# A cached attention block with a dense branch, one core: the first unit of work moves into the loop, and the query weights are loaded at other places

## The chip, the cores and the metric

The kernel runs on one core of one Trainium2 chip. The metric is device time in microseconds (us), the median of several executions. Each run is also profiled once; the profiled execution has its own time, and a span from its first to its last instruction. A core has a matrix engine (PE, with its weight loads as PEld), a vector engine (DVE), an activation engine (ACT), a general engine (POOL) and a queue engine (SP) that issues transfers. Sixteen DMA engines carry out the transfers.

## The reference

Shapes: 8 sequences of one token each, width 512, 32 query heads and 8 key/value heads of 128, 8192 cached positions, hidden width 1792, all in float32.

```python
xn = layernorm(x)                                   # no weights
q  = (xn @ wq) in 32 heads of 128
k, v = each of the 8 cached heads, repeated for 4 query heads
scores = einsum("bhqd,bhkd->bhqk", q, k) * 128 ** -0.5
o  = einsum("bhqk,bhkd->bhqd", softmax(scores), v)  # 8 x 4096
h  = xn @ w1 + b1
act = h * tanh(softplus(h))                         # Mish
out = x + o @ wo + act @ w2
```

The caches are 268 MB each; with `wq`, `wo`, `w1` and `w2` the core has to read about 561 MB.

## The kernel before

**Units.** A unit is one sequence `b` and one pair `m` of key/value heads. There are 32, with `m` outside and `b` inside: unit number `u = 8*m + b`. Each has 8 MiB of keys and 8 MiB of values, loaded by one transfer each, 64 KiB to each of 128 partitions. In the program the work of a unit is:

- `scores`: 32 matmuls of the unit's keys with `wk` (queries spread over the partitions by `key_weights`), in two halves. Between the halves SP is given the load of the next unit's keys.
- `softmax` (DVE, ACT and one small PE matmul), then `values`: 32 matmuls on the values of the unit *before*, with its probabilities `pt8`; then SP is given the load of this unit's values.
- `key_weights` for the next unit, `turn` (PE and DVE bring the probabilities into the layout of `pt8`), and `merge` (the output of the unit before is put into `oT`).

**Places.** All of it goes through one tile, `kv`, of 2.5 rows of 64 KiB a partition. Values have row 0 (`V_AT`); keys of even units have row 1 (`K_AT[0]`), keys of odd units the stretch from 1.5 to 2.5 (`K_AT[1]`), so the two key places share half a row. A key load can start when the scores have read that shared half, which is why the halves are in another order in odd and even units. A value load can start when `values` is through with row 0. All these transfers are issued by SP, in order, and each waits for its place.

**Query weights.** `wq` comes in four pieces of 2 MiB, one for each `m`, into the tile `ws`. `project` makes the queries of 8 units from it (PE, ACT, DVE), `spread` lays them out (DVE, PE, ACT). Both run in odd units, for the next `m`: `project` in units 5, 13 and 21, `spread` in units 7, 15 and 23. The loads of the pieces (`load_q`) are issued by SP behind the value loads of units 4, 12 and 20.

**Order.** The schedule is written out by hand: instructions stand on each engine's queue in the order of the code. A prelude normalises `x`, projects the first queries, and works unit 0 in straight code, with its keys in the values' place (row 0) and `w1` in row 1; `up`, the first product of the dense branch, stands in it too. Then a loop of 16 passes follows. Pass `t` works the odd unit `2t+1` (`unit(t, 0, more)`) and the even unit `2t+2` (`unit(t, 1, more)`); in the last pass `last()` takes the place of the even unit. Parts that belong to some passes only stand under `tc.If`, which is a test and a jump on every engine. `mish`, the activation, runs in pass 0 with `ws` as scratch.

Of the kernel before, what the change touches and what calls it, by code (L numbers as in the profile page):

```python
# [8 lines left out]
F32 = mybir.dt.float32  # L9
# [4 lines left out]
P = 128  # L14
# [41 lines left out]

V_AT = 0
K_AT = (ROW, ROW + ROW // 2)
W1_AT = ROW
W2_AT = 2 * ROW  # L60
PLACES = 2 * ROW + ROW // 2

# [4 lines left out]

LOOPS = UNITS // 2  # L70
FAR = 3.0e38


# [3 lines left out]
def kernel(  # L77
# [72 lines left out]
    for lo in range(0, FG, FG // 2):  # L150
        hi = lo + FG // 2
        nc.scalar.dma_start(b1_sb[:, lo:hi], b1.rearrange("(g f) -> g f", g=G)[:, lo:hi])
    nc.sync.dma_start(kv[:, V_AT : V_AT + ROW], kT[:NB].rearrange("j p f -> (j p f)").rearrange("(p f) -> p f", p=P))
    w1_t = kv[:, W1_AT : W1_AT + 7168].rearrange("p (i f) -> p i f", i=W1R)


# [153 lines left out]
            nc.scalar.copy(qr[:, at].rearrange("p i c -> p (i c)"), X[:, half])  # L310

    wk = const.tile([P, DI, 2, NH * G, REP], F32, name="wk")
    lsel = const.tile([P, 2, H2], F32, name="lsel")
    qT = const.tile([P, H2 * B], F32, name="qT")

# [11 lines left out]
            )  # L327


    def scores(j, k, first, part):  # L330

        w = wk
        lo = 0 if first else DI // 2
        kk = k.rearrange("p (i c f) -> p i c f", i=DI, c=HALF)
        for n in range(DI // 2):
            i = lo + n
            for c in range(HALF):
                nc.tensor.matmul(  # L338
                    S[64 * c : 64 * (c + 1), :],
                    w[:, i].rearrange("p d k h -> p (d k h)"),  # L340
                    kk[:, i, c, :],
                    start=(part == 0 and n == 0),
                    stop=(part == 1 and n == DI // 2 - 1),
                )

    E, RT = {}, {}

    def softmax(j):
        nm = work.tile([P, 1], F32, name="nm")
# [11 lines left out]
    def turn(j):  # L361
        e = E.pop(j)
        for g in range(4):
            nc.tensor.matmul(X[:, g], perm[:, g], e, start=True, stop=True)  # L364
        if j % 2 == 1:

            n = 2 * H2
            nc.tensor.matmul(  # L368
                M[:, 136 : 136 + n], ones, lsel.rearrange("p u h -> p (u h)"), start=True, stop=True
            )  # L370
            rt = work.tile([P, 2, H2], F32, name="rt")
            nc.vector.reciprocal(rt.rearrange("p u h -> p (u h)"), M[:, 136 : 136 + n])  # L372
            RT[0], RT[1] = rt[:, 0], rt[:, 1]
        for tl in range(TL):
            nc.vector.transpose(  # L375
                tr.rearrange("p (l t) c -> p t l c", t=TL)[:, tl],
                X.rearrange("p g (t q l) -> p t l g q", t=TL, q=PP)[:, tl],
            )
        t = tr.rearrange("p y (k z) -> p y k z", k=2)
        nc.vector.tensor_add(t[:, :, 0], t[:, :, 0], t[:, :, 1])  # L380
        for d in range(2):
            half = slice(64 * d, 64 * (d + 1))
            t = tr[half].rearrange("p y (g c h) -> p g y c h", g=4, c=HALF)
            nc.vector.tensor_add(  # L384
                pt8[half, :, :, d * REP : (d + 1) * REP].rearrange("p c y h -> p y c h"),
                t[:, 0],
                t[:, 1],
            )


    def values(vt):
        for n in range(NJ):
            l, c = divmod(n, HALF)
            q = n % G
            nc.tensor.matmul(  # L395
                O[Q * q : Q * (q + 1), :],
                pt8[:, c, TL * l : TL * (l + 1), :].rearrange("p t h -> p (t h)"),
                vt[:, 512 * n : 512 * (n + 1)],
                start=(n < G),
                stop=(n >= NJ - G),  # L400
            )
        os = work.tile([P, DH], F32, name="os")
        nc.vector.tensor_scalar(os, O[:, :DH], isel[:, 0:1], None, op0=ALU.mult)  # L403
        for i in range(1, TL):
            nc.vector.scalar_tensor_tensor(  # L405
                os, O[:, DH * i : DH * (i + 1)], isel[:, i : i + 1], os, op0=ALU.mult, op1=ALU.add
            )
        return os

    def merge(os, u, b):  # L410
        nc.tensor.matmul(M[:, 168 : 168 + H2], os, hsel, start=True, stop=True)  # L411
        nc.vector.tensor_mul(oT[:, :, b], M[:, 168 : 168 + H2], RT[u])

    def turn_o(m):

# [35 lines left out]
                )  # L451

    def mish(flat):
        a, z, z2, one, h = (flat[:, FG * i : FG * (i + 1)] for i in range(5))
        nc.vector.tensor_copy(h, hp)
        nc.vector.scalar_tensor_tensor(a, h, -1.0, h, op0=ALU.mult, op1=ALU.max)
# [22 lines left out]
        turned = flat[:, 5 * FG : 6 * FG]  # L479
# [41 lines left out]
    nc.sync.dma_start(w1_t, w1.rearrange("j p f -> (j p f)").rearrange("(p i f) -> p i f", p=P, i=W1R))  # L521
    project(work.tile([P, 512], F32, name="e", bufs=1))
    spread()
    key_weights(0, 2)
    x_turn()

    def place(at):
        return kv[:, at : at + ROW]
# [6 lines left out]

    def load(name, at, m, b):
        nc.sync.dma_start(place(at), units[name][m, b])  # L537

    load("k", K_AT[1], 0, 1)
    scores(0, place(V_AT), True, 0)  # L540
    scores(0, place(V_AT), False, 1)
    softmax(0)
    load("v", V_AT, 0, 0)
    key_weights(1)
    up(w1_t, b1_sb)
    turn(0)

    def last():

# [11 lines left out]
            nc.sync.dma_start(t, w2_rows[:, a:z])  # L561
            w2_t.append(t)

        os = values(place(K_AT[0]))
        for m in range(NP):
            if m == 1:
                merge(os, 1, B - 1)
                turn_o(NP - 1)
            outputs(m, w_o[m])
        down_long(w2_t[0])  # L570
# [9 lines left out]
            )  # L580
        for p, t in zip(parts[1:], w2_t[1:]):
            down(p[0], p[1], t, p[2], p[3])
        res = work.tile([P, DH], F32, name="os")
        nc.vector.tensor_add(res, O[:, :P], xres)  # L584
        nc.sync.dma_start(out, res)

    def unit(t, p, more):

        j = 1 + p
        scores(j, place(K_AT[(1 + p) % 2]), p == 0, 0)  # L590
        if p == 0:
            with tc.If(t < LOOPS - 1) as here:
                load("k", K_AT[0], (2 * t + 2) // B % NP, (2 * t + 2) % B)
            with here.Else():
                load("v", K_AT[0], NP - 1, B - 1)
        else:
            load("k", K_AT[1], (2 * t + 3) // B % NP, (2 * t + 3) % B)
        scores(j, place(K_AT[(1 + p) % 2]), p == 1, 1)
        softmax(j)
        os = values(place(V_AT))  # L600
        if p == 0:
            with tc.If(t % 4 == 0):
                turn_o((t // 4 + NP - 1) % NP)
            with tc.If(t < LOOPS - 1):
                load("v", V_AT, (2 * t + 1) // B % NP, (2 * t + 1) % B)
            with tc.If(more == 3):  # L606
                spread()
        else:
            load("v", V_AT, (2 * t + 2) // B % NP, (2 * t + 2) % B)
        key_weights((2 * t + 2 + p) % B)  # L610
        if p == 0:
            with tc.If(more == 2):  # L612
                project(tr.rearrange("p y c -> p (y c)")[:, :512])
        else:
            with tc.If(more == 1):
                load_q((t // 4 + 1) % NP)
        turn(j)
        merge(os, p, (2 * t + p) % B)
        if p == 0:
            with tc.If(t == 0):  # L620
                mish(ws[:, : 6 * FG])

    with tc.For_i(0, LOOPS, hint_engines=(), iteration_sync="reg_based") as t:
        more = t % 4 + (t // 12) * 4
        unit(t, 0, more)
        with tc.If(t < LOOPS - 1) as here:
            unit(t, 1, more)
        with here.Else():
            last()

# [37 lines left out]
```

## Time and profile before

| what | value |
|---|---|
| median of 3 runs | 1308.38 us (1307.18 to 1312.3) |
| profiled execution, its own time | 1310.03 us |
| its span | 1308.2 us |
| granted PE clock, mean over the span | 0.866 of full |
| PE busy | 1009.7 us (77%) |
| DVE busy | 359.4 us (27%) |
| DMA share of the 16 engines by SP's queue (q1) | 99.2% |
| moved | 561.43 MB, mean 429 GB/s |

In the views, "L338" is line 338 of the kernel, "SPq" a transfer that SP issues, and what stands in brackets behind an instruction is how long its engine had been idle and what released it. "us to landing" counts from the issue of a transfer to its end. The DMA share of a stretch is the mean over the 16 engines; packets are put to the stretch in which they start, so a short stretch can have a share over 1.

### The profile page before, as it was taken

How to read it: one execution, taken by the hardware profiler on the slowest of the kernel's cores; microseconds unless marked ns; L12 is line 12 of the kernel's file. 1: busy time of each engine (PE TensorE's matmuls, PEld its weight loads, DVE VectorE, ACT ScalarE, POOL GpSimd, SP SyncE). 2: the span in 40 equal slices, each digit the busy share in tenths (PEclk: the TensorE clock that was granted, in tenths of full speed). 3: DMA queues.
4: the chain of work that ended last, by engine and by line, in shares of the span. 5: the costliest groups of instructions: out<-in, count | busy, mean ns of one | idle time of the engine just before them, and what ended most of it. 6: DMA issues, size and time to landing. Idle time of an engine off the chain costs nothing. (4 is left out here: it accounts for less than half of the span.)

```text
span 1308.2 us, 14161 instructions
## 1 busy us (share of the span) xinstructions
PE 1009.7 (77%) x4948; PEld 356.0 (27%) x4948; DVE 359.4 (27%) x654; ACT 39.3 (3%) x89; POOL 2.3 (0%) x10
## 2 busy tenths in 40 slices
PE   5888787777878778687797868779688777778676
PEld 2232232222323222232132323223222222223222
DVE  3235032140323322123131323312233240323312
ACT  1000000000000000000000000000000000000000
POOL 0000000000000000000000000000000000000000
PEclk9999798797898898788798988788888898988888
DMA  9999999999999999999999999999999999999998
GB/s 406 444 420 434 435 425 438 428 438 433 427 425 439 428 435 431 433 433 434 425 423 423 443 419 447 419 447 419 447 421 447 423 443 427 439 431 435 435 419 351
DMA packets 11719, 561.43 MB, mean 429 GB/s; under 512 B 1312, under 2 KB 1704, under 8 KB 1968
## 3 DMA queue, kind: packets, MB, share of 16 engines
q1 hardware_dynamic: 11536, 560.03, 99.2%
q10 hardware_dynamic: 160, 1.06, 0.2%
q8 instruction: 19, 0.31, 0.1%
q14 instruction: 4, 0.03, 0.0%
HBM read 561.01 MB, written 0.07 MB: 429 GB/s over the span
## 5 line engine op out<-in xcount | busy, mean ns | idle before, releaser
L338 PE MATMUL s<-kv,wk 128*64 128x512 f32 x2048 | 532.0, 662 | 178.3 <-DMA kv<-in_kT 101.4
L338 PEld LDWEIGHTS s<-kv,wk 128*64 128x64 f32 x2048 | 182.2, 151 | 493.0 <-issue 414.0
L395 PE MATMUL o<-kv,pt 128*32 128x512 f32 x2048 | 256.1, 658 | 27.2 <-DMA kv<-in_v 22.4
L350 DVE TENSOR_REDUCE nm<-s 128x1 f32<-128x512 f32 x32 | 22.1, 692 | 540.9 <-issue 366.6
L364 PE MATMUL x<-e,perm 128*128 128x512 f32 x256 | 133.6, 670 | 18.0 <-PEq L612 16.0
L395 PEld LDWEIGHTS o<-kv,pt 128*32 128x32 f32 x2048 | 66.9, 120 | 192.7 <-issue 161.9
L375 DVE STREAM_TRANSPOSE tr<-x 128x512 f32<-128x512 f32 x128 | 80.3, 685 | 9.0 <-PE x L364 7.0
L364 PEld LDWEIGHTS x<-e,perm 128*128 128x128 f32 x256 | 51.9, 214 | 97.2 <-issue 90.5
L321 DVE TENSOR_TENSOR wk<-qr,mask 128x1024 f32<-128x1024 f32 (+1 forms) x34 | 64.8, 1906 | 32.1 <-DVEq L606 15.4
L403 DVE TENSOR_SCALAR os<-o,isel 128x128 f32<-128x128 f32 x32 | 11.2, 351 | 225.7 <-PE o L395 200.8
L358 ACT ACTIVATE e<-s,nmx 128x512 f32<-128x512 f32 x32 | 22.0, 687 | 1110.5 <-DVE nmx L355 1110.5
L384 DVE TENSOR_TENSOR pt<-tr 64x512 f32<-64x512 f32 x64 | 43.9, 686 | 2.2
L380 DVE TENSOR_TENSOR tr<-tr 128x1024 f32<-128x1024 f32 x32 | 39.2, 1225 | 1.1
L351 PE MATMUL m<-ident,nm 128*128 128x128 f32 x64 | 18.1, 370 | 26.2 <-DVE nm L350 26.2
L405 DVE SCALAR_TENSOR_TENSOR os<-o,isel,os 128x128 f32<-128x128 f32 x96 | 33.7, 351 | 3.4
L351 PEld LDWEIGHTS m<-ident,nm 128*128 128x128 f32 x64 | 11.1, 218 | 65.4 <-DVE nm L350 65.4
L303 PE MATMUL x<-tr,gwide 128*128 128x512 f32 x16 | 14.5, 1007 | 13.4 <-DVE tr L298 10.5
L275 PE MATMUL h<-ws,xn 128*8 128x512 f32 x64 | 12.0, 835 | 6.0 <-PEq L606 5.1
L359 DVE TENSOR_SCALAR lsel<-rsel,l 128x8 f32<-128x8 f32 x32 | 7.4, 231 | 29.8 <-ACT e L358 29.8
L411 PE MATMUL m<-hsel,os 128*128 128x8 f32 x64 | 10.9, 242 | 5.7 <-DVE rt L372 5.6
L372 DVE RECIPROCAL rt<-m 128x16 f32<-128x16 f32 x16 | 4.1, 258 | 40.4 <-PE m L368 40.4
L353 DVE TENSOR_TENSOR far<-m,apart 128x128 f32<-128x128 f32 x32 | 9.3, 291 | 21.0 <-PE m L351 21.0
(103 smaller groups left out, 156.4 us busy)
## 6 DMA issues: line engine op xcount, KB each, us to landing
kv<-in_wo SPq DMA_DIRECT2D x4, 2048.0 KB, 19.9
ws<-in_wq SPq DMA_DIRECT2D x3, 2048.0 KB, 33.4
kv<-in_w SPq DMA_DIRECT2D x1, 3584.0 KB, 35.4
kv<-in_w SPq DMA_DIRECT2D x2, 1024.0 KB, 27.8
ws<-in_wq ACTq DMA_DIRECT2D x1, 1024.0 KB, 5.1
ws<-in_wq SPq DMA_DIRECT2D x1, 1024.0 KB, 7.2
kv<-in_w SPq DMA_DIRECT2D x1, 768.0 KB, 26.4
kv<-in_kT SPq DMA_DIRECT2D x32, 29.0
```

Of the source, the lines that this page charges most:

```text
L303: nc.tensor.matmul(X[:, half], gwide, masked[:, at].rearrange("p i c -> p (i c)"), start=True, stop=True,)
L321: nc.vector.tensor_mul(w[:, i : i + n], q[:, i : i + n].to_broadcast([P, n, 2, NH * G, REP]), mask.rearrange("p (o d k r) -> p o d k r", o ...
L338: nc.tensor.matmul(S[64 * c : 64 * (c + 1), :], w[:, i].rearrange("p d k h -> p (d k h)"), kk[:, i, c, :], start=(part == 0 and n == 0), s ...
L350: nc.vector.tensor_reduce(nm, S, axis=AX.X, op=ALU.max, negate=True)
L351: nc.tensor.matmul(M[:, 0:P], nm.to_broadcast([P, P]), ident, start=True, stop=True)
L358: nc.scalar.activation(e, S, AF.Exp, bias=nmx, accum_out=l)
L364: nc.tensor.matmul(X[:, g], perm[:, g], e, start=True, stop=True)
L375: nc.vector.transpose(tr.rearrange("p (l t) c -> p t l c", t=TL)[:, tl], X.rearrange("p g (t q l) -> p t l g q", t=TL, q=PP)[:, tl],)
L380: nc.vector.tensor_add(t[:, :, 0], t[:, :, 0], t[:, :, 1])
L384: nc.vector.tensor_add(pt8[half, :, :, d * REP : (d + 1) * REP].rearrange("p c y h -> p y c h"), t[:, 0], t[:, 1],)
L395: nc.tensor.matmul(O[Q * q : Q * (q + 1), :], pt8[:, c, TL * l : TL * (l + 1), :].rearrange("p t h -> p (t h)"), vt[:, 512 * n : 512 * (n ...
L405: nc.vector.scalar_tensor_tensor(os, O[:, DH * i : DH * (i + 1)], isel[:, i : i + 1], os, op0=ALU.mult, op1=ALU.add)
```

## The change

Unit 0 is no longer straight code. The loop has 17 passes; pass `t` works the odd unit `2t-1` (`odd(t)`, skipped in pass 0) and then the even unit `2t` (`even(t)`, or `last()` in pass 16). In pass 0 the even unit skips `values` and `merge`, and `up` stands there under a test.

- The first keys go to `K_AT[0]`, the place that keys of even units always have, and `w1` goes to row 0: the two change places. The loads of unit 1's keys and of unit 0's values, which stood in the prelude, are now those of the even unit in pass 0.
- `load_q` runs before the loop for `m = 1` (SP waits for `project` of `m = 0`, which reads the same tile), and in the even units 6 and 14 for `m = 2` and `m = 3`. `project` and `spread` stay in the units where they were.
- `mish` stays in unit 1; its scratch is `tr` in place of `ws`, and it reads the hidden values straight from PSUM. `os` and `rt` are tiles of one buffer each instead of two.

```diff
-W1_AT = ROW
+W1_AT = 0
...
-LOOPS = UNITS // 2
+LOOPS = UNITS // 2 + 1
...
-    nc.sync.dma_start(kv[:, V_AT : V_AT + ROW], kT[:NB].rearrange(...))
+    nc.sync.dma_start(kv[:, K_AT[0] : K_AT[0] + ROW], kT[:NB].rearrange(...))
...
     project(work.tile([P, 512], F32, name="e", bufs=1))
     spread()
+    load_q(1)
     key_weights(0, 2)
     x_turn()
...
-    load("k", K_AT[1], 0, 1)
-    scores(0, place(V_AT), True, 0)
-    scores(0, place(V_AT), False, 1)
-    softmax(0)
-    load("v", V_AT, 0, 0)
-    key_weights(1)
-    up(w1_t, b1_sb)
-    turn(0)
...
+    def odd(t):
+        k = place(K_AT[1])
+        scores(k, True, 0)
+        with tc.If(t < LOOPS - 1) as here:
+            load("k", K_AT[0], t // 4 % NP, 2 * t % B)
+        with here.Else():
+            load("v", K_AT[0], NP - 1, B - 1)
+        scores(k, False, 1)
+        softmax(1)
+        values(place(V_AT))
+        with tc.If(t % 4 == 1):
+            turn_o((t // 4 + NP - 1) % NP)
+        with tc.If(t < LOOPS - 1):
+            load("v", V_AT, (2 * t + 2 * UNITS - 1) // B % NP, (2 * t + B - 1) % B)
+        with tc.If(t % 4 + t // (LOOPS - 1) == 0):
+            spread()
+        key_weights(2 * t % B)
+        with tc.If(t % 4 - t // (LOOPS - 2) == 3):
+            project(tr.rearrange("p y c -> p (y c)")[:, :512])
+        turn(1)
+        merge(0, (2 * t + B - 2) % B)
+        with tc.If(t == 1):
+            mish(tr.rearrange("p y c -> p (y c)"))
+
+    def even(t):
+        k = place(K_AT[0])
+        scores(k, False, 0)
+        load("k", K_AT[1], t // 4 % NP, (2 * t + 1) % B)
+        scores(k, True, 1)
+        softmax(0)
+        with tc.If(t > 0):
+            values(place(V_AT))
+        key_weights((2 * t + 1) % B)
+        with tc.If(t == 0):
+            up(w1_t, b1_sb)
+        load("v", V_AT, t // 4 % NP, 2 * t % B)
+        with tc.If(t % 4 - t // B * 4 == 3):
+            load_q((t // 4 + 2) % NP)
+        turn(0)
+        with tc.If(t > 0):
+            merge(1, (2 * t + B - 1) % B)
+
     with tc.For_i(0, LOOPS, hint_engines=(), iteration_sync="reg_based") as t:
-        more = t % 4 + (t // 12) * 4
-        unit(t, 0, more)
+        with tc.If(t > 0):
+            odd(t)
         with tc.If(t < LOOPS - 1) as here:
-            unit(t, 1, more)
+            even(t)
         with here.Else():
             last()
```

**The start on SP.** These are SP's rows from the start to the loop, first before, then now; `kv<-in_w` is `w1`, `ws<-in_wq` a piece of the query weights.

```order
L142 DMA kv<-in_x 8x512
L146 DMA ws<-in_wq 128x2048
L153 DMA kv<-in_kT 128x16384
L521 DMA kv<-in_w 128x7168
L537 DMA kv<-in_kT 128x16384
L537 DMA kv<-in_v 128x16384
L623 COMPARE_AND_BRANCH
```

```order
L142 DMA kv<-in_x 8x512
L146 DMA ws<-in_wq 128x2048
L153 DMA kv<-in_kT 128x16384
L523 DMA kv<-in_w 128x7168
L136 DMA ws<-in_wq 128x4096
L625 COMPARE_AND_BRANCH
```

The keys of unit 1 and the values of unit 0 have left the straight code, and the second piece of the query weights has come into it; the first four transfers keep their order.

**The even unit on SP.** These are SP's rows from the key load of the even unit to `load_q`, first before, then now. L615 before and L619 now are the tests around `load_q`.

```order
L537 DMA kv<-in_kT 128x16384
L537 ISA x2
L537 DMA kv<-in_v 128x16384
L615 ISA
L615 COMPARE_AND_BRANCH
REGISTER_ALU
L136 ISA
L136 DMA ws<-in_wq 128x4096
```

```order
L540 DMA kv<-in_kT 128x16384
L613 COMPARE_AND_BRANCH
L613 UNCONDITIONAL_BRANCH x2
L616 COMPARE_AND_BRANCH
L616 UNCONDITIONAL_BRANCH x2
L540 ISA x2
L540 DMA kv<-in_v 128x16384
L619 ISA
L619 COMPARE_AND_BRANCH
REGISTER_ALU
L136 ISA
L136 DMA ws<-in_wq 128x4096
```

The tests of `values` and `up` now stand between the two loads; `load_q` keeps its place behind the value load, under a test that other passes fulfil.

**From the odd to the even unit on PE.** These are PE's rows from the last test of the odd unit to the `values` of the even one (`s` are the scores, `o<-kv,pt_93` is `values`), first before, then now.

```order
L620 COMPARE_AND_BRANCH
L620 UNCONDITIONAL_BRANCH x2
L626 COMPARE_AND_BRANCH
L338 REGISTER_ALU
L338 MATMUL s<-kv,wk 64x512 x32
L351 REGISTER_ALU
L351 MATMUL m<-ident,nm 128x128
L395 REGISTER_ALU
L395 MATMUL o<-kv,pt_93 32x512 x32
```

```order
L603 COMPARE_AND_BRANCH
L603 UNCONDITIONAL_BRANCH x2
L626 REGISTER_ALU
L626 UNCONDITIONAL_BRANCH
L628 COMPARE_AND_BRANCH
L343 ISA
L343 MATMUL s<-kv,wk 64x512 x32
L356 REGISTER_ALU
L356 MATMUL m<-ident,nm 128x128
L613 COMPARE_AND_BRANCH
L398 REGISTER_ALU
L398 MATMUL o<-kv,pt_93 32x512 x32
```

Ahead of the even unit's scores there is one jump more, out of the test `t > 0`; ahead of its `values` there is one test more.

More of the change, by code (lines that the diff above doesn't have):

```diff
@@ L152 @@
         nc.scalar.dma_start(b1_sb[:, lo:hi], b1.rearrange("(g f) -> g f", g=G)[:, lo:hi])
-    nc.sync.dma_start(kv[:, V_AT : V_AT + ROW], kT[:NB].rearrange("j p f -> (j p f)").rearrange("(p f) -> p f", p=P))
+    nc.sync.dma_start(
+        kv[:, K_AT[0] : K_AT[0] + ROW],
+        kT[:NB].rearrange("j p f -> (j p f)").rearrange("(p f) -> p f", p=P),
+    )
     w1_t = kv[:, W1_AT : W1_AT + 7168].rearrange("p (i f) -> p i f", i=W1R)
@@ L312 @@
     wk = const.tile([P, DI, 2, NH * G, REP], F32, name="wk")
+    os = const.tile([P, DH], F32, name="os")
+    rt = const.tile([P, 2, H2], F32, name="rt")
     lsel = const.tile([P, 2, H2], F32, name="lsel")
@@ L327, in key_weights, with scores @@
             )
-    def scores(j, k, first, part):
+    def scores(k, first, part):
         w = wk
@@ L344, in scores @@
                 )
-    E, RT = {}, {}
+    E = {}
     def softmax(j):
@@ L370, in turn @@
             )
-            rt = work.tile([P, 2, H2], F32, name="rt")
             nc.vector.reciprocal(rt.rearrange("p u h -> p (u h)"), M[:, 136 : 136 + n])
-            RT[0], RT[1] = rt[:, 0], rt[:, 1]
         for tl in range(TL):
@@ L401, in values @@
             )
-        os = work.tile([P, DH], F32, name="os")
         nc.vector.tensor_scalar(os, O[:, :DH], isel[:, 0:1], None, op0=ALU.mult)
@@ L407, in values, with merge @@
             )
-        return os
-    def merge(os, u, b):
+    def merge(u, b):
         nc.tensor.matmul(M[:, 168 : 168 + H2], os, hsel, start=True, stop=True)
-        nc.vector.tensor_mul(oT[:, :, b], M[:, 168 : 168 + H2], RT[u])
+        nc.vector.tensor_mul(oT[:, :, b], M[:, 168 : 168 + H2], rt[:, u])
     def turn_o(m):
@@ L453, in mish @@
     def mish(flat):
-        a, z, z2, one, h = (flat[:, FG * i : FG * (i + 1)] for i in range(5))
-        nc.vector.tensor_copy(h, hp)
-        nc.vector.scalar_tensor_tensor(a, h, -1.0, h, op0=ALU.mult, op1=ALU.max)
+        h = hp
+        a, z, z2, one = (flat[:, FG * i : FG * (i + 1)] for i in range(4))
+        nc.vector.tensor_copy(a, h)
+        nc.vector.scalar_tensor_tensor(a, a, -1.0, a, op0=ALU.mult, op1=ALU.max)
         nc.scalar.activation(z, a, AF.Exp, scale=-1.0)
@@ L478, in mish @@
             )
-        turned = flat[:, 5 * FG : 6 * FG]
+        turned = z
         nc.vector.transpose(turned, act)
@@ L562, in last @@
             w2_t.append(t)
-        os = values(place(K_AT[0]))
+        values(place(K_AT[0]))
         for m in range(NP):
             if m == 1:
-                merge(os, 1, B - 1)
+                merge(1, B - 1)
                 turn_o(NP - 1)
@@ L582, in last @@
             down(p[0], p[1], t, p[2], p[3])
-        res = work.tile([P, DH], F32, name="os")
+        res = os
         nc.vector.tensor_add(res, O[:, :P], xres)
         nc.sync.dma_start(out, res)
[L587 to L621, printed above, removed]
```

## The prediction

> **What bounds the kernel now.** I read the page's totals first, then the stretches of the span, then SP's transfers one by one.
>
> The page's first, DMA and issue rows:
>
> ```profile
> span 1308.2 us, 14161 instructions
> DMA packets 11719, 561.43 MB, mean 429 GB/s; under 512 B 1312, under 2 KB 1704, under 8 KB 1968
> ws<-in_wq SPq DMA_DIRECT2D x3, 2048.0 KB, 33.4
> ```
>
> Stretches of the span (us, busy time and instructions of PE, PEld, DVE, ACT and POOL, granted clock, DMA share, GB/s):
>
> ```profile
> 0.00:5.00 5.00, 0.00 (x0) 0.00 (x0) 2.41 (x6) 2.21 (x4) 2.29 (x10) 1.00 0.65 223
> 5.00:70.00 65.00, 50.27 (x232) 18.54 (x234) 18.90 (x54) 4.81 (x9) 0.00 (x0) 0.95 1.02 442
> 200.00:1200.00 1000.00, 775.33 (x3684) 273.66 (x3678) 267.13 (x467) 26.47 (x62) 0.00 (x0) 0.86 1.00 432
> 1270.00:1303.30 33.30, 24.34 (x226) 9.49 (x222) 11.30 (x23) 0.58 (x1) 0.00 (x0) 0.90 0.94 395
> 1303.30:1308.20 4.90, 1.04 (x24) 0.63 (x24) 0.29 (x1) 0.00 (x0) 0.00 (x0) 0.77 0.05 14
> ```
>
> The 16 DMA engines are full from 5 us on, at 432 GB/s over a thousand microseconds. What is not full is short: at 432 GB/s the first stretch loses 5.0 x (1 - 223/432) = 2.4 us, the last but one 33.3 x (1 - 395/432) = 2.9 us, and the end, where the last products and the output follow the last transfer, 4.9 us. The change moves the same bytes, so the time can only change where the DMA engines run dry. SP's queue has to be asked how near to that it comes. A key or value load that is issued while the one ahead of it is still under way costs nothing; I call the time from its issue to the landing of the one ahead its lead.
>
> The rows are, unit by unit, the value load and the next key load, in the units with `project` (5, 13, 21) and then in those with `spread` (7, 15, 23): start, length, queue, line. Behind them stand the times from issue to landing of the six value loads, in that order.
>
> ```profile
> 246.67 0.33 SPq L537 DMA_DIRECT2D kv<-in_v  x1
> 268.51 0.34 SPq L537 DMA_DIRECT2D kv<-in_kT  x1
> 560.56 0.33 SPq L537 DMA_DIRECT2D kv<-in_v  x1
> 582.39 0.34 SPq L537 DMA_DIRECT2D kv<-in_kT  x1
> 878.29 0.33 SPq L537 DMA_DIRECT2D kv<-in_v  x1
> 901.82 0.34 SPq L537 DMA_DIRECT2D kv<-in_kT  x1
> 328.78 0.33 SPq L537 DMA_DIRECT2D kv<-in_v  x1
> 350.02 0.34 SPq L537 DMA_DIRECT2D kv<-in_kT  x1
> 645.62 0.33 SPq L537 DMA_DIRECT2D kv<-in_v  x1
> 667.09 0.34 SPq L537 DMA_DIRECT2D kv<-in_kT  x1
> 958.86 0.33 SPq L537 DMA_DIRECT2D kv<-in_v  x1
> 981.27 0.34 SPq L537 DMA_DIRECT2D kv<-in_kT  x1
> ```
>
> ```profile
> kv<-in_v SPq DMA_DIRECT2D x1, 29.4
> kv<-in_v SPq DMA_DIRECT2D x1, 31.6
> kv<-in_v SPq DMA_DIRECT2D x1, 29.6
> kv<-in_v SPq DMA_DIRECT2D x1, 24.7
> kv<-in_v SPq DMA_DIRECT2D x1, 24.1
> kv<-in_v SPq DMA_DIRECT2D x1, 26.4
> ```
>
> Unit 5: the values land at 246.67 + 29.4 = 276.1, the key load is issued at 268.5, a lead of 7.6 us. In the same way unit 13 has 9.8, unit 21 has 6.1, unit 7 has 3.5, unit 15 has 2.6 and unit 23 has 4.0. `spread` has the short leads, since its layout work stands between `values` and the next scores.
>
> What a short lead costs is seen in two passes: the first contains unit 13, the second unit 15, and the third unit 7.
>
> ```profile
> 540.80:619.40 78.60, 60.90 (x300) 22.52 (x298) 20.65 (x36) 2.73 (x6) 0.00 (x0) 0.87 1.00 432
> 619.05:697.60 78.55, 64.03 (x290) 21.95 (x288) 21.71 (x37) 2.73 (x6) 0.00 (x0) 0.85 0.98 421
> 306.05:384.60 78.55, 61.61 (x288) 21.34 (x284) 21.72 (x37) 2.73 (x6) 0.00 (x0) 0.87 1.00 428
> ```
>
> With a lead of 2.6 the share falls to 0.98: 0.02 x 78.55 = 1.6 us are lost. With 3.5 it stays at 1.00, and 428 against 432 GB/s is at most 0.7 us; with 9.8 nothing. So the DMA engines begin to run dry at a lead of about 3.5, 2.6 costs 1.6, and I count one microsecond more for each one less.
>
> **The change part by part.**
>
> *The query weights.* A piece is 2048 KB, 2.1 MB, at 429 GB/s 4.9 us. Before, it lay on the queue behind the values of units 4, 12 and 20: the transfers of the following `project` unit landed 4.9 us later than without it, and PE had that time for `project`. Now the pieces lie ahead of the loop and behind the values of units 6 and 14. The cushion leaves the `project` units and comes to the `spread` units 7 and 15; unit 23 has none in either kernel. PE's path from one landing to the key load after it stays the same, so 4.9 is taken off the leads of units 5, 13 and 21, and added in 7 and 15:
>
> - unit 5: 7.6 - 4.9 = 2.7, costs 1.6;
> - unit 13: 9.8 - 4.9 = 4.9, costs nothing;
> - unit 21: 6.1 - 4.9 = 1.2, costs 1.6 + 1.4 = 3.0;
> - unit 15: 2.6 + 4.9 = 7.5, gives back 1.6; unit 7: 8.4, gives back 0.7 at most;
> - unit 23: 4.0 as before.
>
> Sum: +4.6 - 2.3 = +2.3 us. A load that was hidden anyway has lent its time to its neighbour; that is the term on which this prediction rests. The bounds: 0 for the lost leads if PE's path is 2 us shorter there than in these three instances (it varies by 3.7 us among them), and +4.6 with 2 us more in each of units 5 and 21.
>
> *The start.* Its rows are the issue of `w1`, its time to landing, the stretch of unit 0's scores that the first half takes (34 of 64 PE records), `up`, and the first scores behind the loop's entry:
>
> ```profile
> 2.08 0.74 SPq L521 DMA_DIRECT2D kv<-in_w  x1
> kv<-in_w SPq DMA_DIRECT2D x1, 3584.0 KB, 35.4
> 27.89:37.30 9.41, 9.41 (x34) 3.27 (x36) 1.00 1.01 433
> 46.32 6.20 PE L445 MATMUL h<-kv,oX 128*8 128x448 f32 x64
> 60.94 16.91 PE L338 MATMUL s<-kv,wk 128*64 128x512 f32 x64 [4.79 <-DVEq L623]
> ```
>
> `w1` lands at 37.5 us and the second piece of query weights, now behind it, at 42.4. SP waits for the first `project` before it issues that piece, and SP has nothing else to issue until then. The keys of unit 1 now wait for the half of unit 0's scores, 37.3 us: lead 5.1, free. The entry into the loop now stands ahead of these scores. Behind `turn` it left PE idle for 4.79 us; here PE has 3 us of waiting for the first keys to hide it, and if all of the rest came through, the lead would be 3.3 and the cost about 0.7. I take 0. The values of unit 0 now wait for `up`, which ends at 52.5; with a test they are issued at some 54, while unit 1's keys, 19.6 us at 429 GB/s, land at 62: lead 8, free. After that the queue is 4.9 us longer than before until unit 4, which is no gain, since it was not dry there.
>
> *The tests.* The rows are PE's longest wait for its own sequencer at such tests (us in total, times, longest), the scores' group with its waits, and the scores of an even unit:
>
> ```profile
> PE x L364 <- PEq L612: 16.0, 10, 2.1
> L338 PE MATMUL s<-kv,wk 128*64 128x512 f32 x2048 | 532.0, 662 | 178.3 <-DMA kv<-in_kT 101.4
> 261.38 10.95 PE L338 MATMUL s<-kv,wk 128*64 128x512 f32 x50 [0.20 <-issue]
> ```
>
> In the even unit PE passes three tests more (`values`, `up`, `merge`), and one at the loop's head. Between 0.2 us (two tests ahead of line 338) and 2.1 us for each, a pass has 0.8 to 8.4 us more on PE. The nearest row is that of skipped tests, 1.6 us for several in a row. The cover is PE's wait for keys, 101.4 us in 18 waits, 5.6 each; so 0. From the odd to the even unit only one jump is added, and there is no cover in units 5, 21 and 23: 0.2 us each on the short leads, +0.4 with unit 23 still above 3.5.
>
> The Trainium skill ("Runtime: NRT & Kernel Launch", Instruction fetch mechanics) says that a taken branch out of the fetched window waits for a fetch of its page, and gives that as a reason against runtime control flow; the jump over a skipped body would be such. No row here gives a page's fetch by itself; the 2.1 us is the longest wait of that kind, and the second rival below takes it as the price.
>
> *The rest.* `mish` keeps its 16 DVE instructions; two of them read PSUM now. `os` and `rt` with one buffer are rewritten a unit after they are read. Work that PE or DVE does there is covered by the same waits for transfers. The end is the same code, issued in the same order: 0.
>
> Sum: 2.3 + 0.4 = +2.7 us on the span, 1310.9. The profiled execution took 1310.03 by its own time, 1.7 above the median of the runs; against the median, 1308.38 + 2.7 = **1311 us**, 0.2% more. A measurement of this kernel can tell about 0.5%, 6.5 us, from no change, so this is a forecast of no change.
>
> **The rivals.**
>
> *Nothing runs dry.* The leads of units 5 and 21 stay above 3.5, because PE's path is shorter in other executions. For it: unit 13 did the same work with a lead 2.2 to 3.7 us longer. Against it: two of three units came out short. Then only the 2.3 us of units 7 and 15 are gained: 1306. Also no change.
>
> *The jump is dear.* Leaving the test `t > 0` costs 2.1 us in front of the even unit's scores, in each pass. It decides from 1.4 us on, where unit 23's lead falls to 2.6. Then units 5 and 21 cost 1.9 us more each, unit 23 1.6 + 0.7 and unit 13 (lead 2.8) 1.4: 2.7 + 3.8 + 2.3 + 1.4 = 10.2, 1318.6 us, slower. Against it: two tests cost 0.20 at that place.
>
> *The load ahead pays.* `project` is freed of a wait for its weights, and the leads grow everywhere. It would have to win more than 6.5 of the 11.8 us in which the engines are not full (2.4 + 2.9 + 4.9 + 1.6), and nothing in the change touches the first three; 1301 us at the best. In the trace `project` waits 5.1 us in all, and for PE's sequencer:
>
> ```profile
> PE h L275 <- PEq L606: 5.1, 3, 1.7
> ```
>
> **How the numbers follow.** The forecast has 0.60, nothing dry 0.28, the dear jump 0.09, the load ahead 0.03. The likeliest is 1311. The range goes down to the second case and up over the bounds of the first (+4.6 and 0.7 at the start on top of 2.7 would be 1316): 1306 to 1316. Faster by over 0.5% is the last case, 0.03; slower the third, 0.09; the rest, 0.88, is no change.
>
> **What would show it.** DMA share in the stretches from unit 5 to unit 8 and from 21 to 24 falls by 0.02 to 0.04, and stays at 1.00 around unit 15; the leads computed as above are 2 to 3 us in unit 5, 1 to 2 in unit 21 and over 7 in units 7 and 15. The first scores start within 2 us of 27.9, and SP issues unit 1's keys near 37.5. It would be wrong if the share were under 0.98 in passes without `project` or `spread`, if SP issued unit 1's keys after 41 us, or if PE stood over 1.4 us in front of the even unit's scores in each pass.

## The result, and the profile after

The changed kernel takes 1318.3 us (median of 6 runs, 1317.4 to 1322.9), the kernel before 1308.5 beside it: a ratio of 1.0076, 95% interval 1.0057 to 1.0095. It is slower by some 10 us where 1311, and no change, was forecast. The profiled execution has a span of 1316.5 us against 1308.2, 8.3 us more; these 8.3 us are what the traces have to explain.

Totals from the page of the changed kernel:

```profile
span 1316.5 us, 15368 instructions
DMA packets 11713, 561.33 MB, mean 426 GB/s; under 512 B 1312, under 2 KB 1704, under 8 KB 1968
```

Stretches of its span, the same as before (the last ends later, with the kernel), and among them the three stretches from the landing of unit 4's, 12's and 20's values to the key load behind `project`:

```profile
0.00:5.00 5.00, 0.00 (x0) 0.00 (x0) 2.41 (x6) 2.21 (x4) 2.30 (x10) 1.00 0.61 217
5.00:70.00 65.00, 41.66 (x206) 15.87 (x208) 19.01 (x54) 4.81 (x9) 0.00 (x0) 0.95 0.98 418
240.00:277.70 37.70, 31.42 (x152) 12.33 (x154) 10.56 (x19) 1.95 (x4) 0.00 (x0) 0.82 0.97 419
556.10:595.40 39.30, 33.07 (x152) 12.76 (x154) 10.56 (x19) 1.95 (x4) 0.00 (x0) 0.76 0.93 402
873.20:912.80 39.60, 33.38 (x152) 12.84 (x154) 10.56 (x19) 1.95 (x4) 0.00 (x0) 0.76 0.92 399
200.00:1200.00 1000.00, 770.38 (x3722) 279.45 (x3722) 265.36 (x465) 27.25 (x64) 0.00 (x0) 0.88 1.00 430
1270.00:1312.00 42.00, 32.99 (x302) 12.93 (x294) 11.50 (x24) 1.04 (x3) 0.00 (x0) 0.88 0.94 399
```

The stretches of the three `project` units in the kernel before:

```profile
232.00:268.50 36.50, 31.23 (x150) 11.94 (x152) 10.58 (x19) 1.95 (x4) 0.00 (x0) 0.78 1.02 443
548.10:582.40 34.30, 29.11 (x150) 11.70 (x152) 10.59 (x19) 1.95 (x4) 0.00 (x0) 0.85 1.03 446
863.90:901.80 37.90, 32.76 (x150) 12.47 (x152) 10.59 (x19) 1.95 (x4) 0.00 (x0) 0.75 1.04 449
```

The bytes move more slowly at two kinds of place: ahead of 70 us (418 GB/s where 442 stood) and in the three `project` units (share 0.92 to 0.97, where 1.02 to 1.04 stood). The reasoning about leads applies to both. The rows of SP for units 5, 13 and 21, and the time from issue to landing of the three value loads:

```profile
253.08 0.34 SPq L540 DMA_DIRECT2D kv<-in_v  x1
277.66 0.34 SPq L540 DMA_DIRECT2D kv<-in_kT  x1
570.87 0.34 SPq L540 DMA_DIRECT2D kv<-in_v  x1
595.35 0.34 SPq L540 DMA_DIRECT2D kv<-in_kT  x1
888.13 0.34 SPq L540 DMA_DIRECT2D kv<-in_v  x1
912.76 0.34 SPq L540 DMA_DIRECT2D kv<-in_kT  x1
```

```profile
kv<-in_v SPq DMA_DIRECT2D x1, 26.2
kv<-in_v SPq DMA_DIRECT2D x1, 24.4
kv<-in_v SPq DMA_DIRECT2D x1, 24.2
```

The leads are 1.6, -0.1 and -0.4 us. From here on leads go by the end of the last packet in the trace's packet records, as the expectations below do; that is 0.3 to 0.5 us less: 1.3, -0.5 and -0.8 here, and 7.1, 9.3 and 5.6 in the kernel before. Units 7 and 15 now have 8.9 and 8.5, unit 23 has 3.5 as before.

At the start, PE's last row of the prelude and the first scores of unit 0 in the timeline:

```profile
24.28 0.61 PE L251 MATMUL m<-kv,ident 8*8 8x128 f32 x8
32.17 15.73 PE L343 MATMUL s<-kv,wk 128*64 128x512 f32 x64 [7.28 <-PEq L626]
```

In the list of PE's waits (total, times, longest) the two that are new:

```profile
PE s L343 <- DVE tr L378: 8.1, 12, 0.7
PE s L343 <- PEq L626: 7.3, 1, 7.3
```

The keys had landed at 27.4 us, but the scores start at 32.2: PE's own sequencer stands at line 626, the loop's test `t > 0`, whose jump leads over the whole body of `odd`. The records of PE's sequencer (PEldq) for this line show how long (its 17 branches: shortest, median and longest in ns, start of the first and the last in us):

```profile
L626 PEldq COMPARE_BRANCH  x17: 73/83/6737, 24.5 to 1237.7; - x17
```

The one jump, from 24.5 to 31.3 us, takes 6.7 us; where the test falls through it takes about 0.08. The other new wait is the 0.7 us (0.2 before) between `turn` and the even unit's scores in each pass. SP's rows of the second piece of query weights and of unit 1's keys, and the time to landing of the first:

```profile
14.96 0.33 SPq L136 DMA_DIRECT2D ws<-in_wq  x1
41.51 0.36 SPq L540 DMA_DIRECT2D kv<-in_kT  x1
```

```profile
ws<-in_wq SPq DMA_DIRECT2D x1, 2048.0 KB, 27.3
```

The piece lands at 42.3 us and unit 1's keys are issued at 41.5, 4 us later than forecast, with the queue all but empty; the packets show a gap of 2.1 us. (A gap here and below is idle time in the packet records, as a mean over the 16 engines.)

**Where the 8.3 us are.** At the landing of the values of units 5, 6, 13, 14, 21, 22 and 31 both kernels have moved the same bytes. By the last packet of each, the changed kernel is behind by 3.4, 4.5, 3.2, 5.6, 4.5, 7.4 and 7.5 us, and by 8.3 at the end. So the start costs 3.4, units 5, 13 and 21 cost 1.2, 2.5 and 2.9, the stretches between give back 1.4 and 1.1 (units 7 and 15 among them), and the end takes 0.8. Of the 3.4 at the start the gap is 2.1. Most of the rest lies between the landing of unit 1's keys and of its values, where the same bytes take 59.7 us in place of 58.2 without a gap; the cause of that is open.

### The profile page after: what moved, and what is told of

Same layout as the page of the kernel before. It is cut to its first block, busy times and chain, and to the rows that moved or that the text cites. A ratio compares the mean times of both kernels' runs of the same rounds, so it can differ in the third digit from the quotient of the medians.

```text
span 1316.5 us, 15368 instructions
## 1 busy us (share of the span) xinstructions
PE 1001.9 (76%) x4948; PEld 363.3 (28%) x4948; DVE 360.6 (27%) x654; ACT 39.3 (3%) x89; POOL 2.3 (0%) x10
## 5 line engine op out<-in xcount | busy, mean ns | idle before, releaser
L343 PE MATMUL s<-kv,wk 128*64 128x512 f32 x2048 | 525.8, 654 | 167.7 <-DMA kv<-in_kT 75.2
L343 PEld LDWEIGHTS s<-kv,wk 128*64 128x64 f32 x2048 | 182.2, 149 | 475.9 <-issue 393.0
L398 PEld LDWEIGHTS o<-kv,pt 128*32 128x32 f32 x2048 | 73.4, 119 | 183.8 <-issue 182.4
L356 PE MATMUL m<-ident,nm 128*128 128x128 f32 x64 | 16.2, 338 | 32.2 <-DVE nm L355 32.2
L383 DVE TENSOR_TENSOR tr<-tr 128x1024 f32<-128x1024 f32 x32 | 39.2, 1225 | 1.1
```

What stands on the lines that cost most here:

```text
L343: nc.tensor.matmul(S[64 * c : 64 * (c + 1), :], w[:, i].rearrange("p d k h -> p (d k h)"), kk[:, i, c, :], start=(part == 0 and n == 0), s ...
L356: nc.tensor.matmul(M[:, 0:P], nm.to_broadcast([P, P]), ident, start=True, stop=True)
L398: nc.tensor.matmul(O[Q * q : Q * (q + 1), :], pt8[:, c, TL * l : TL * (l + 1), :].rearrange("p t h -> p (t h)"), vt[:, 512 * n : 512 * (n ...
```

## The experiments

A table of all runs stands behind them.

**Query weights back.** Theory A is two separate losses (cushion and entry), theory B a price of the tests in every pass.

```diff
-    load_q(1)                                    # ahead of the loop
...
-        with tc.If(t % 4 - t // B * 4 == 3):      # even units 6, 14
-            load_q((t // 4 + 2) % NP)
+        with tc.If(t % 4 + t // 12 * 4 == 2):     # even units 4, 12, 20
+            load_q((t // 4 + 1) % NP)
```

> The changed kernel with only the query weights put back: no piece ahead of the loop, the pieces again behind the values of units 4, 12 and 20. Nothing of the computation is left out. Theory A (two causes: the 4.9 us piece no longer stands ahead of project's units, and the loop's entry makes unit 1's keys late once): the leads of units 5, 13 and 21 come back by 4.9 us each, from 1.3, -0.5 and -0.8 to about 6.2, 4.4 and 4.1, and the 7.5 us lost there are won back; units 7 and 15 fall to 4.0 and 3.6, which costs 0 to 1 us. At the start the queue is now 4.9 us shorter (w1 lands near 36.9), while unit 1's keys are still issued at about 41.5 us: the DMA engines stand for some 5.5 us there in place of 2.6. Sum 1318.3 - 7.5 + 0.5 + 3 = 1314 us. Theory B (the tests and jumps cost PE in every pass, and the place of the query weights doesn't matter): the three units stay dry, the start gets 3 us worse, 1321 us.

1318.4 us, ratio 1.0081 (1.0065 to 1.0097): theory A's sum was missed. Its part on the leads came out, its price of the start did not. The leads of units 5, 13 and 21 are 4.2, 10.6 and 6.0, and none of them loses anything now. What was won there is lost at the start, which costs 7.6 us more than in the changed kernel, not 3. A stretch of its span, and SP's issue of unit 1's keys:

```profile
30.00:50.00 20.00, 16.90 (x66) 5.88 (x66) 0.69 (x1) 0.00 (x0) 0.00 (x0) 1.00 0.66 272
```

```profile
42.11 0.36 SPq L539 DMA_DIRECT2D kv<-in_kT  x1
```

`w1` has landed at 36.7, so the queue is dry for 6.4 us until the first packets, 1 us behind the issue; the packets show a gap of 7.5, and a second one of 1.3 follows a short lead (2.5) of unit 2's keys. That lead is short because of another long jump of PE, of 8.2 us, from the end of unit 0 over the code of `last`: it ends at 73.1, while unit 1's keys had landed at 65.1. The piece ahead of the loop had been hiding most of the late entry.

**Ahead in the kernel before.** The same move of the query weights, without the new loop.

```diff
+    load_q(1)                                    # ahead of the loop
...
-            with tc.If(more == 1):                # even units 4, 12, 20
-                load_q((t // 4 + 1) % NP)
+            with tc.If(t % 4 + t // 8 * 4 == 2):  # even units 6, 14
+                load_q((t // 4 + 2) % NP)
...
-                mish(ws[:, : 6 * FG])
+                mish(tr.rearrange("p y c -> p (y c)"))
```

> The kernel before with only the query weights loaded ahead: one piece ahead of the loop, the next behind the values of units 6 and 14 (mish uses the place that it has in the changed kernel, so that the piece doesn't overwrite it). Loop, first loads and unit 0 stay as before. Nothing of the computation is left out. Theory A (the cushion was the cover of project): leads of units 5, 13 and 21 fall by 4.9 us from 7.6, 9.8 and 6.1 to about 2.7, 4.9 and 1.2, or 1 to 4 us less where the clock falls otherwise; units 7 and 15 rise over 7; no loss at the start. Two or three short leads cost 3 to 7.5 us and 1.6 come back: 1310 to 1314 us. Theory B (the new loop's jumps alone make the three units late): no loss, 1306.5 to 1308.4 us.

1309.4 us, ratio 1.0010 (0.9997 to 1.0023), just under the range. The leads fall to 0.1, 4.4 and 1.8, about as theory A and the prediction had them (2.2, 4.4 and 0.7 in this measure), and unit 5 loses 1.8 us; units 7 and 15 rise to 8.3 and 8.8 and lose nothing. The cushion was real: theory B, which had no loss in these units, is refuted by the leads. By itself the move of the query weights costs 0.7 us by the medians, which the interval does not tell from nothing; what it costs in one unit it gives back in another.

**Unit 0 straight.** The loop entry and the tests are taken out; the query weights stay ahead.

```diff
+    # unit 0: scores, load of unit 1's keys, softmax, up, load of its values, turn
+    with tc.For_i(1, LOOPS, ...) as t:
+        odd(t)
-    with tc.For_i(0, LOOPS, ...) as t:
-        with tc.If(t > 0):
-            odd(t)
...
-        with tc.If(t > 0):                        # also ahead of merge; up without its test
-            values(place(V_AT))
+        values(place(V_AT))
```

> The changed kernel with unit 0 in straight code ahead of a loop of 16 passes, without the four tests for the first pass; the query weights and the first loads stay as in the changed kernel. Nothing of the computation is left out. Theory A (the one long branch over the odd unit's body at the loop's first pass makes unit 1's keys late): the first scores start near 28 us in place of 32.2, unit 1's keys are issued near 37.5 with a lead of about 4, the start's 2.6 us come back; the jump into even scores falls from 0.7 to 0.2 us, which gives units 5, 13 and 21 0.45 us each. The three units stay short of their cushion: 1318.3 - 2.6 - 1.4 = 1314.3 us. Theory C (not the branch but the new order of the first loads holds the first scores back): first scores still at 32 us, at most 1.4 us won, 1317 us. Theory B (the tests and jumps cost PE in every pass): all of it comes back, 1308 us.

1311.0 us, ratio 1.0017 (1.0006 to 1.0027): 7 us are back, more than theory A had. The first scores, and SP's issue of unit 1's keys:

```profile
27.92 16.68 PE L343 MATMUL s<-kv,wk 128*64 128x512 f32 x64 [3.06 <-DMA kv<-in_kT]
```

```profile
37.82 0.33 SPq L540 DMA_DIRECT2D kv<-in_kT  x1
```

PE waits for the keys again, not for its sequencer, and unit 1's keys are issued at 37.8, where the prediction had them. At unit 5's values the kernel is 4.6 us ahead of the changed one. The leads are 1.8, 3.9 and 2.5, and units 5, 13 and 21 lose 1.5, 0.2 and 1.6 where they lost 1.2, 2.7 and 2.9. Theory C (the order of the first loads holds the scores back) is refuted; theory B in its strong form too, since 2 us and two short leads stay.

**Layout work in even units.** `project` and `spread` move out of the units that have lost their cushion.

```diff
-        with tc.If(t % 4 + t // (LOOPS - 1) == 0):     # in odd(t)
-            spread()
-        with tc.If(t % 4 - t // (LOOPS - 2) == 3):
-            project(tr...)
+        with tc.If(t % 4 + t // 12 * 4 == 2):          # in even(t), ahead of turn
+            project(tr...)
+        with tc.If(t % 4 + t // 12 * 4 == 3):
+            spread()
```

> The changed kernel with project moved from units 5, 13 and 21 into the even units 4, 12 and 20, and spread from units 7, 15 and 23 into units 6, 14 and 22, where it stands right behind the piece of query weights on the queue's clock. Nothing of the computation is left out. Theory A (project needs 4.9 us more than an odd unit without the piece leaves it; even units lack the wait for values that holds up the last score products of odd units, about 4 to 5 us): project's units keep leads of 3 us or more, the 7.5 us lost in units 5, 13 and 21 come back, the start's 2.6 us stay: 1311 us. Rival (project drains the queue wherever it stands without the piece ahead): units 4, 12 and 20 are dry in their place, 1318 us.

1311.9 us, ratio 1.0032 (1.0020 to 1.0044): as theory A had it. `project`'s units have leads of 6.5, 7.8 and 7.7, no unit behind the start loses anything, and what is left of the loss is the start (a gap of 3.1 us).

**Both.** Unit 0 straight and the layout work in even units.

> Unit 0 in straight code and the layout work (project, spread) in the even units, both together, on the changed kernel. Nothing of the computation is left out. Theory A (one long branch at the loop's entry, and three odd units without their cushion, are two separate losses): the two gains, 7.4 us for the straight unit 0 and 6.5 us for the even units, overlap in units 5, 13 and 21, since the straight form had already brought most of that back; the start's 3 us come off the 1311.9 us of the kernel with the layout work in even units: 1308 to 1309 us, no lead under 3 us anywhere, so about the kernel before. Rival (one cause for both, the loop's first pass): no more than the better of the two, 1311 us.

1306.2 us, ratio 0.9984 (0.9975 to 0.9993), faster than both kernels by a little, and better than expected. No lead is under 4 us. Its totals, and its long middle, which ran at 432 GB/s before:

```profile
span 1304.3 us, 14078 instructions
DMA packets 11706, 561.21 MB, mean 430 GB/s; under 512 B 1312, under 2 KB 1704, under 8 KB 1968
```

```profile
105.00:1200.00 1095.00, 852.15 (x4091) 296.10 (x4089) 298.61 (x521) 28.84 (x68) 0.00 (x0) 0.87 1.00 433
```

Its 12 runs lie between 1305.85 and 1306.49, the 32 of the kernel before beside it between 1305.74 and 1312.82. The fastest runs of the two are alike. It would fit that in some executions of the kernel before nothing runs dry and in others its short leads do, but only one of them was profiled, so this is not shown.

**Even unit first.** The loop is turned, so that nothing is jumped over at its entry; the tests inside the even unit stay.

```diff
-    with tc.For_i(0, LOOPS, ...) as t:
-        with tc.If(t > 0):
-            odd(t)
-        with tc.If(t < LOOPS - 1) as here:
-            even(t)
-        with here.Else():
-            last()
+    with tc.For_i(0, LOOPS - 1, ...) as t:
+        even(t)
+        odd(t + 1)
+    last()
```

> The changed kernel with the loop turned: 16 passes of an even and then an odd unit, and the end behind the loop. The tests on values, up and merge stay in the even unit; only the jump over the odd unit's body and the test of the last pass are gone. Nothing of the computation is left out. Theory A1 (the first pass's jump over the long odd body is what PE's sequencer waits for): first scores within 1 us of the keys' landing at 27.4, unit 1's keys at about 37.6, the start's 2.6 us come back; with the jump gone the leads of units 5, 13 and 21 are as in the straight form, 1.8, 3.9 and 2.5: 1310 to 1312 us. Theory A2 (entering any code of the loop for the first time costs it): first scores still near 32, 1313 to 1315 us. Theory B (the tests inside the even unit cost PE in every pass): still over 1316 us.

1311.5 us, ratio 1.0021 (1.0010 to 1.0033): the number of theory A1, by another way. The first scores and the first products behind the loop in PE's timeline, PE's waits for values, and SP's first loads of the end:

```profile
28.07 16.43 PE L343 MATMUL s<-kv,wk 128*64 128x512 f32 x64 [3.02 <-DMA kv<-in_kT]
...
1273.78 1.93 PE L398 MATMUL o<-kv,pt 128*32 128x512 f32 x8 [5.91 <-PEq L662]
```

```profile
PE o L398 <- DMA kv<-in_v: 59.7, 29, 4.1
```

```profile
1273.60 1.99 SPq L548 DMA_DIRECT2D kv<-in_wo  x4
```

Entering the loop costs nothing where no body is jumped over: A1 holds, A2 doesn't. Up to the last values (1271.2 us) the kernel is level with the 1306.2 us kernel, leads of 6.4, 6.2 and 9.2 among it. Then it leaves the loop for `last`, PE stands 5.9 us, SP issues the first output weights only at 1273.6, 2.4 us after the last values, and the packets show a gap of 4.8.

This is not the price of a jump: no branch of PE takes over 1 us in this kernel. It is the loop's end, at which the engines wait for each other. SP's waits at the loop's line (625), and a wait of PE in the kernel before:

```profile
SPq L625 <- DMA kv<-in_v: 26.9, 2, 19.3
SPq L625 <- DVEq L603: 1.1, 1, 1.1
```

```profile
PE o L395 <- DVE pt L384: 4.8, 1, 4.8
```

SP issued the last values at 1242.7 and then stood until they had landed and DVE was through (1272.8); the semaphores' records show all engines released at 1273.5. In the kernel before, where `last` stands inside the loop, SP issues the first output weights at 1265.3. Most of PE's 5.9 us is no loss of this kernel: for 4.7 of them DVE's `turn` was not done, and the kernel before waits 4.8 us for it too.

The leads are better than in the straight form for a reason that no theory had. In the other kernels PE's list has "PE s L343 <- DMA kv<-in_v" (line 338 in the kernel before, 60.2 us in 15 times): the last scores of an odd unit wait for the values of the unit ahead, which they don't read. With `last` behind the loop this wait is gone from the list, and only `values` waits for values. That it comes from `last`, whose loads go to the same place, is inferred.

**The changed kernel again**, unaltered, for a second profile.

> The changed kernel once more, unaltered, for a second profile. If the clock's phase in units 5, 13 and 21 belongs to the kernel's own rhythm, their leads come out within 0.5 us of 1.3, -0.5 and -0.8, and the DMA engines stand at the same four places for the same times. If it is chance in each execution, the leads scatter by 3 us and more, as they did from kernel to kernel, while the branch at the start takes 6.7 us again.

1316.2 us, ratio 1.0065 (1.0045 to 1.0085). The start is the same:

```profile
32.22 13.29 PE L343 MATMUL s<-kv,wk 128*64 128x512 f32 x50 [7.38 <-PEq L626]
```

The leads are 5.6, 1.0 and -0.9. Unit 21 repeats to 0.1 us, unit 13 is off by 1.5 and unit 5 by 4.3. Neither theory holds alone. Unit 5 took 37.6 us from landing to key load at a granted clock of 0.82 in the first profile, and 33.1 at 0.93 in this one. Units 5 and 13 lose 2.6 us less here, and the span is 2.1 us shorter.

**Straight, query weights back.** What is left of the change is the swapped first loads and the loop's new cut.

> Unit 0 in straight code and the query weights at their old places, on the changed kernel: what is left of the change is the new order of the first loads and the loop's new cut. Nothing of the computation is left out. Theory A: units 5, 13 and 21 have leads of 6 us or more, unit 15 about 3. But at the start w1 lands near 36.4 and unit 1's keys, which wait for half of unit 0's scores, are issued at 37.8 us, 1.4 us after it: the DMA engines stand for about 3 us. So the piece of query weights ahead of the loop had been the cover of the swapped first loads: 1310 to 1312 us, no better than with the pieces ahead. Rival (the swap of the first loads is free): 1308 us.

1311.1 us, ratio 1.0021 (1.0007 to 1.0034), theory A. The leads are 6.7, 8.9 and 7.5. SP's issue of `w1` and of unit 1's keys, and the time to landing of `w1`:

```profile
2.08 0.72 SPq L523 DMA_DIRECT2D kv<-in_w  x1
37.17 0.33 SPq L539 DMA_DIRECT2D kv<-in_kT  x1
```

```profile
kv<-in_w SPq DMA_DIRECT2D x1, 3584.0 KB, 35.4
```

The keys are issued about when `w1` has landed, and the packets show a gap of 3.1 us. The swap of the first loads alone is not free: it needs the piece of query weights ahead of the loop.

**`w1` behind the entry**, to see what the jump waits for.

```diff
-    nc.sync.dma_start(w1_t, ...)                  # ahead of the loop
-    load_q(1)
...
         load("k", K_AT[1], t // 4 % NP, (2 * t + 1) % B)
+        with tc.If(t == 0):
+            nc.sync.dma_start(w1_t, ...)
+            load_q(1)
```

> The changed kernel with the loads of w1 and of the second piece of query weights issued in the first pass, behind unit 1's keys, in place of ahead of the loop. Nothing of the computation is left out. PE still takes the same jump over the odd unit's body at about 24.5 us, but the DMA queue is empty from the landing of the first keys, 27.4 us, until PE has done half of unit 0's scores. Theory D (the jump waits for code that is fetched behind the data packets of full DMA engines): the fetch is through soon after 27.4, first scores at 28 to 29.5 us, PE's wait 3 to 4.5 us in place of 7.3. Theory E (the fetch takes its 6.7 us whatever the DMA engines do): first scores at 32 us again. Either way the DMA engines stand idle from 27.4 to about 38 us, and the time is 5 to 10 us over that of the changed kernel.

PE's last row of the prelude and the first scores:

```profile
24.16 0.61 PE L251 MATMUL m<-kv,ident 8*8 8x128 f32 x8
30.30 15.70 PE L343 MATMUL s<-kv,wk 128*64 128x512 f32 x64 [5.53 <-PEq L627]
```

PE's wait is 5.5 us in place of 7.3, and the jump itself 5.0 in place of 6.7, between the two theories: 1.8 us of it go with a queue that is empty from 27.4 us on, and most of it stays. The packet records say what the jump waits for. They have packets of a kind of their own, "instruction". In the changed kernel one of 16 KB begins 4.3 us after the start of the jump, takes 1.0 and ends 1.4 us before the jump does; here one begins 2.4 us after it, takes 1.3 and ends 1.3 us before. That the fetch stood behind data packets is likely from this, but not shown further. The one run took 1340.9 us, 22.6 over the changed kernel and far more than expected. I had counted the gap at the start (13.6 us) but not that `up` then waits 21.9 us for `w1`, which holds up unit 0's values for a second gap of 6.2.

**All of them**, but for the last, which ran once. Losses are taken against the kernel of 1306.2 us: how much later the values of unit 5 land (274.5 there), how much longer it takes from the values of unit 5 to those of 6, of 13 to 14 and of 21 to 22 (38.7 each there), and how much later the last values land (1271.2 there).

| kernel | median, us | start, to unit 5 | units 5 / 13 / 21 | last values |
|---|---|---|---|---|
| before | 1308.5 | 1.1 | 0 / 0.2 / 0 | 3.9 |
| changed | 1318.3 | 4.5 | 1.2 / 2.7 / 2.9 | 11.4 |
| changed, again | 1316.2 | 4.8 | 0 / 1.3 / 2.9 | 9.3 |
| query weights back | 1318.4 | 12.1 | 0 / 0 / 0 | 13.0 |
| ahead in the kernel before | 1309.4 | -0.2 | 1.8 / 0 / 0.3 | 2.3 |
| unit 0 straight | 1311.0 | -0.1 | 1.5 / 0.2 / 1.6 | 4.0 |
| layout work in even units | 1311.9 | 5.2 | 0 / 0 / 0 | 5.4 |
| straight and even units | 1306.2 | 0 | 0 / 0 / 0 | 0 |
| even unit first | 1311.5 | 0 | 0 / 0 / 0 | 0 |
| straight, query weights back | 1311.1 | 3.5 | 1.1 / 0 / 0 | 7.4 |

The kernel before beside these runs took 1308.5 to 1308.7 us. The 1.1 of unit 5 in the last row, at a lead of 6.7, and the 1.1 of the kernel before at the start are not explained by a lead.

## Why the prediction was wrong

**What bounds the kernel** was right. The large entries of the table are places where SP's next load comes late, and the two kernels without one are level up to the last values.

**The start is the step that failed.** The prediction put the entry into the loop at 4.79 us at most, hid 3 us of it behind the wait for the first keys, and took 0 with a bound of 0.7. It had that price from the entry of the loop before, which falls straight into its body. The new entry is a jump over the body of `odd`. It takes PE's sequencer 6.7 us, and PE is idle for 7.3. The rest followed as written: scores 4.3 us late, unit 1's keys at 41.5 in place of 37.5, which the prediction had named as a sign of being wrong, and a lead of 0.7 by landing in place of 5.1. It costs 3.4 us against the kernel before. Shown by the straight unit 0 (keys at 37.8) and by the even unit first (scores at 28.1), each of which takes the jump away.

**The price of a jump stood in the trace before.** The prediction says that no row gives it, and took 2.1 us as the longest wait of that kind. It had looked in the list of waits, and there a wait is put down to what ended last. The sequencer's records of line 626 of the kernel before, the test for `last`, have it:

```profile
L626 PEldq COMPARE_BRANCH  x31: 68/169/7927, 93.5 to 1276.8; - x31
```

Seven of these 31, one in each of the first seven passes, take 5.7 to 7.9 us: PE jumps from the end of the even unit over the code of `last`. Behind six of them the wait is put down to the next keys, which landed later still, so they cost nothing there. At the new entry the cover was 3 us.

**The query weights**: the mechanism was right, its size was not. In units 5, 13 and 21 it was to cost 4.6, and 6.6 were measured, the jump's share included; it was to give back 2.3, and it gave 2.5. Two errors stand behind this, of opposite signs. The leads were 0.9, 4.9 and 1.5 us shorter than forecast, since PE's path was longer. On the other hand the price rule was too steep: over all runs a lead of 1.8 to 2.5 cost 0.3 to 1.6 us, which holds its 1.6 at 2.6, but -0.5 and -0.8 cost 2.7 and 2.9, where one microsecond more for each less makes 4.3 and 4.6.

**PE's path** in these units is the second step that failed: the prediction let it stay the same. The path is the time from the landing of the values ahead of the unit to the key load behind it: 36.5, 34.3 and 38.0 us in the kernel before. Over the four kernels without the jump at the entry (before, ahead in it, and the two straight ones with the layout work in odd units) the 12 instances have a mean of 36.2; over the three profiles with it (the changed kernel twice, query weights back) 9 instances lie between 32.9 and 39.6, with a mean of 37.4. Unit 13 was no chance find: it has 34.3 to 34.9 us in all four kernels without that jump, each time at a granted clock of 0.85. In the three profiles with it, it has 39.2 us (0.76), 37.7 (0.82) and 32.9 (0.93). What moves the clock there is not shown.

**The tests** were covered, as forecast. The jump between odd and even unit adds 0.5 us in each pass (0.7 against 0.2), where the prediction added 0.2 in units 5 and 21. The other 0.7 us of the longer mean path are not explained by any run, and with instances 6 us apart they may be chance; the granted clock in the three units is 0.82, 0.76 and 0.76 against 0.78, 0.85 and 0.75 before.

**The rest and the end**: 0.8 us at the end where 0 was forecast, not followed up.

**The rivals.** "The jump is dear" gave 1318.6 us, which is close by luck, and not by its mechanism: it wanted 2.1 us in front of the scores in every pass, and there are 0.7 in each and 7.3 once. The rule behind it was the right one, of the Trainium skill ("Runtime: NRT & Kernel Launch", Instruction fetch mechanics): a taken branch out of the fetched window waits for the fetch of its target. The traces agree: in all runs together PE has 31 jumps of 5.0 to 8.2 us, and each of them ends 1.2 to 1.5 us after the end of an instruction packet of 16 KB. It need not be the first time that the target is run, as the seven passes of the kernel before show; why there are none in its later passes is open. "Nothing runs dry" gave 1306; the two repairs together are that case, at 1306.2. "The load ahead pays" is refuted: the time rose, and that best kernel with the pieces ahead is only 2.5 us under the kernel before.

## What to carry to other kernels

Where transfers set the time, give each load its lead from the trace, and look for what stands ahead of it on the queue: a transfer that looks like work to be hidden can be the cover of a slow step behind it. Here the swapped first loads cost nothing at the start with a piece of query weights ahead of the loop and 3.5 us without it, and the same piece had been the cover of `project`. Take a path's length from several executions before resting on a margin of a few microseconds, and prefer the order with leads of 4 us or more everywhere: it won little in the median here, but brought the scatter from 7 us to 0.6.

Take the price of a jump from the sequencer's records of its line, not from the list of waits, which hides it wherever something else ends later. Put a jump over a long body where PE waits anyway. Loads for the work behind a loop are better issued inside it: at the loop's end SP stood until the last transfer had landed.

## What the runs showed of the hardware

- PE's jump over the body of `odd` at the loop's entry took 6.7 to 6.9 us in four profiles with the DMA engines full, and 5.0 when their queue was empty for the last 2 us of it. ACT and DVE were past the same jump after 0.5 and 0.6 us. In later passes the way from the odd to the even unit takes PE 0.7.
- Each of the 31 jumps of PE that took 5 us or more ended 1.2 to 1.5 us after a 16 KB packet of instructions. Seven are in the kernel before, where PE's other waits cover them.
- At the end of a loop with more work behind it the engines waited for each other and for the last transfer: SP was held until 1273.5 us, 2.3 us after the last values.
- The granted clock moves the same stretch of work in the same unit of the same kernel from 37.6 us (0.82) to 33.1 us (0.93) between two executions.
- A queue that has run dry shows its first packets about 1 us after the issue, in the packet records.
